# One network's first product by Strassen's scheme, in tiles of 256 tokens

## The chip, the cores and the metric

The kernel runs on one core of one Trainium2 chip. The metric is device time in microseconds (us) of one execution. Before the change three runs gave 991.76, 989.52 and 991.64 us; the median is 991.64 us.

## The reference

Attention over 4 x 576 = 2304 tokens gives x of 2304 x 512, and two networks follow it.

```python
# attention: a pooled part (factor 4) plus a local part (|i - j| < 4), summed
x = (out_up + out_local).transpose(0, 2, 1, 3).reshape(2304, 512)
# first network, 1536 wide
g = x @ w_gate
x = (g / (1 + exp(-g)) * (x @ w_val)) @ w_out
# second network, 2048 wide
h = np.maximum(x @ w_in, 0.0)
out = h * h @ w_out
```

The weights arrive as 64-bit floats and every product is to have about fp32 accuracy.

## The kernel before

Every operand of a product is split into a high and a low part (tiles `w`, `xh`, `hh`, type fp32r), and one product of a 128-row block is three matmuls: high by high, high by low, low by high. `proj` (lines 929 to 931) does the first products of both networks, with a block of weights as the stationary operand and the tokens of a tile as the moving one: 4 row blocks x 3 = 12 matmuls for one block of 128 columns. `down` (939 to 941) is the second product of the first network. The second product of the second network (1232 to 1234) holds 128 tokens of `hh` and moves 512 columns of weights.

The work has four stages on TensorE. Attention runs first, woven into the first one below. **B1** does units 0 to 5 of the first network's 12 units (a unit is 128 of the 1536 columns: gate, value, down, 36 matmuls): six tiles of 256 tokens, then two of 384; tiles 0 and 1 do units 4 and 5 later, under the name R. **B2** does units 6 to 11 in six tiles of 384 and adds the partial result that B1 spilled. **C** is the second network: six tiles of 384 tokens by 16 units, 12 matmuls of 384 columns and 9 of 512 in each.

VectorE (DVE) and ScalarE (ACT) turn the 64-bit weights into the two parts (`w_task`, lines 271 to 309: one ACT operation, three DVE operations on bits, one ACT copy, one DVE subtraction, each 128 x 512), split x (892, 898), and do the steps between two products (960 to 982 in the first network; 1212 to 1222 in the second). All loads and spills are issued by SyncE's queue (SP), in the order of its program; a load stands there until its buffer is free.

The order on every engine is fixed when the program is built, by a planner in the code (`Order`): it keeps a clock for each engine, gives every step a cost (`dve`, `act`, `products`, `dma`), and takes next the step that can begin first, by due times where several can. Until its clock says 40 us it puts matmuls on zeros (`fill`, line 1124) where TensorE would have nothing to do. Buffers are counted in `free`; a step that takes one waits in the plan until one is given back.

Of the kernel before, what the change touches and what calls it, by code (L numbers as in the profile page):

```python
# [23 lines left out]
WIN = 64  # L24
# [5 lines left out]
T2 = 384  # L30

X_WIDE = 6
X_AT = [*range(0, X_WIDE * T1, T1), *range(X_WIDE * T1, NTOK + 1, T2)]
NT1 = len(X_AT) - 1
NT2 = NTOK // T2
# [26 lines left out]
def attn_moe_kernel(ctx: ExitStack, tc: tile.TileContext, qT, kT, vw, vin, vp, qp, kp, qs, ks, vs, maskc, masks, identc, wB, wC, out):  # L62
# [60 lines left out]
    class Order:  # L123
        def __init__(self):
            self.flying = []
            self.queues = {k: [] for k in ("x", "qk", "sum", "rows", "v", "att", "w", "mlp", "other")}
            n = {"att": N_ATT, "y": N_Y, "gv": N_GV, "p": N_P, "pt": N_PT, "v": N_V, "xt": N_XT}
            n |= {"wst": N_WST, "wf": N_WF, "w1": NW1, "w2": NW2, "xh": N_XH, "sg": N_SG, "hh": N_HH, "ys": 1}
            self.free = {k: [0.0] * c for k, c in n.items()}
            self.clock = {e: 0.6 for e in "vaptd"}  # L130
            self.load, self.filler, self.streak, self.landed = {}, None, 0.0, 0.0
# [33 lines left out]
        def start(self, task):  # L165
# [7 lines left out]
            for k in set(s.take):  # L173
                slots, n = sorted(self.free[k]), s.take.count(k)
                if len(slots) < n:
                    return None
                t = max(t, slots[n - 1])
# [28 lines left out]
        def run(self):  # L206
            while self.flying or any(self.queues.values()):
# [7 lines left out]
                for k in s.take:  # L215
                    self.free[k].remove(min(self.free[k]))
# [23 lines left out]
                for k in s.give:  # L240
                    self.free[k].append(t)
# [10 lines left out]
    w1_pool = tc.alloc_tile_pool(name="w1", bufs=1, side="right")  # L252
    pools = {"w1": w1_pool}
    w_tiles, w_tasks = {}, {}

    def w_task(key, src, slot, due, cond=None):

        u = {}

        def load():  # L260
            if key[1] == 0:
                w_tiles[key[0]] = pools[slot].tile(
                    [128, 2, 3, 512], F32R, tag=slot, bufs={"w1": NW1, "w2": NW2}[slot], name=slot
                )
            u["hi"], u["lo"] = (w_tiles[key[0]][:, i, key[1], :] for i in range(2))
            u["st"] = com.tile([128, 512, 2], I32, tag="wst", bufs=N_WST, name="wst")
            nc.sync.dma_start(out=u["st"], in_=src)

        def scale():
            u["f"] = com.tile([128, 512], I32, tag="wf", bufs=N_WF, name="wf")  # L270
            nc.scalar.activation(
                out=u["f"].bitcast(F32), in_=u["st"][:, :, 1].bitcast(F32), func=AF.Abs, scale=2.0**-112
            )

        def exponent():
            nc.vector.tensor_scalar(
                out=u["f"],
                in0=u["f"],
# [6 lines left out]
        def sign():  # L285
            nc.vector.scalar_tensor_tensor(
                out=u["f"],
                in0=u["st"][:, :, 1],
                scalar=-0x80000000,
                in1=u["f"],  # L290
                op0=ALU.bitwise_and,
                op1=ALU.bitwise_or,
            )

        def last_bits():
            nc.vector.scalar_tensor_tensor(  # L296
                out=u["f"],
                in0=u["st"][:, :, 0],
                scalar=29,
                in1=u["f"],  # L300
                op0=ALU.logical_shift_right,
                op1=ALU.bitwise_or,
            )

# [3 lines left out]
        def low():  # L308
# [38 lines left out]
    def pool_rows(b, which, half, h):  # L347
        src, dst = (k_t, kd_t) if which == "k" else (q_t, qd_t)
        if b not in dst:

            room = com.tile([128, KD, T2], F32, tag="ys", name="ys").rearrange("p k n -> p (k n)")
# [25 lines left out]
    def pool_v(b):  # L377

        us = [None] * HP

        def load(g):
            if g % 2 == 0:
                new = w1_pool.tile([128, 2, 3, 512], F32R, tag="w1", bufs=NW1, name="w1").bitcast(F32)
                us[g : g + 2] = [new[:QC, i, :2].rearrange("p c n -> p (c n)") for i in range(2)]
# [11 lines left out]
        for g in range(HP):  # L396
            stage = Stage("d", dma(QC * 1024), lambda g=g: load(g), ("w1",) if g % 2 == 0 else ())
            loads.append(Task([stage], x_due(0) - 9.0))
            give = ("w1",) if g % 2 else ()
# [7 lines left out]
    def x_tile(t):  # L407
        if t not in x_t:
            order.free["xt"].remove(min(order.free["xt"]))
            x_t[t] = com.tile([128, KD, T2], F32, tag="xt", bufs=N_XT, name="xt")  # L410
# [83 lines left out]
    def local_task(b, i, ins, due, bls=(0, 1), early=False):  # L494
# [5 lines left out]
        def room(k, size=None):  # L500
            if not early_room:
                early_room.append(com.tile([128, 2 * KD * T2], F32, tag="xh", bufs=N_XH, name="xh"))
            return early_room[0][:, k * 256 : k * 256 + (size or n * WIN)]
# [9 lines left out]
        def scores():  # L513
# [4 lines left out]
            if early:  # L518
                u["p"] = room(2 * i).rearrange("p (c k) -> p c k", k=WIN)
# [50 lines left out]
        def turned():  # L570
            u["pt"] = room(5 + 2 * i) if early else att.tile([128, 512], F32, tag="pt", bufs=N_PT, name="pt")[:, : n * WIN]
# [62 lines left out]
        if early:  # L634
            p_take, pt_take, pt_give = ("xh",) * first, (), ("xh",) * last
# [241 lines left out]
    xh_t, x_tasks, y_t, ys_t, downs = {}, {}, {}, {}, []  # L877

    def x_task(key, n, load=None, cond=None, give=()):
# [9 lines left out]
        def high(k0):  # L889
            if k0 == 0:  # L890
                xh_t[key] = com.tile([128, 2, KD, T2], F32R, tag="xh", bufs=N_XH, name="xh")
            nc.scalar.activation(
# [527 lines left out]
```

## Time and profile before

| what | value |
|---|---|
| median of 3 runs (lowest to highest) | 991.64 us (989.52 to 991.76) |
| span of the profiled execution | 989.6 us |
| TensorE matmul (PE), busy | 976.9 us, 99% |
| VectorE (DVE), busy | 546.8 us, 55% |
| ScalarE (ACT), busy | 371.8 us, 38% |
| mean granted TensorE clock | 0.996 |
| moved by DMA | 100.11 MB |

For the profiled execution there is its span, from the first instruction to the last, and no other time. The lowest run, 989.52 us, is not above it, so nothing can be seen that lies around the span; the median is 2.0 us above it.

A matmul's listed time runs from its start to the modelled end of its results, and the next one starts long before that. How long one really takes is therefore read from the distance between starts. B1 with attention ends at about 287 us, B2 at about 591 us, C at 985 us.

### The profile page before, as it was taken

The page shows a single profiled execution, that of the slowest core. Times are in us where ns is not written, and L with a number is a line of the kernel's source. Part 1 is how long each engine was busy: PE and PEld are TensorE (multiplying, and loading weights), DVE is VectorE, ACT ScalarE, POOL GpSimd, SP SyncE. Part 2 cuts the span into 40 slices and gives each one's busy share as a digit, 9 for nine tenths or more (in the row PEclk, how much of TensorE's full clock was granted, in tenths as well). Part 3 has the DMA queues.
Part 4 walks back from the last instruction along what each step waited for, and adds up shares of the span by engine and source line. Part 5 has one row for each costly group of instructions (what it writes and reads, how often), then busy time and mean ns, then how long its engine had stood idle before and what let it go on. Part 6 is the DMA issues. An engine that isn't in the chain of part 4 may idle for free.

```text
span 989.6 us, 17229 instructions
## 1 busy us (share of the span) xinstructions
PE 976.9 (99%) x7122; PEld 915.8 (93%) x7122; DVE 546.8 (55%) x1163; ACT 371.8 (38%) x844; POOL 23.8 (2%) x31
## 2 busy tenths in 40 slices
PE   8989999999999999999999999999999999999998
PEld 7868999999999999999999999999999999999996
DVE  6999996559589698542342598532322322322222
ACT  3676663443355355221121255432322322322222
POOL 0202020000000000000000000000000000000000
PEclk9989999999999999999999999999999999999999
DMA  9989785142473555220320554010100000000000
GB/s 274 265 269 266 209 185 137 44 123 51 145 251 112 185 183 174 96 90 7 96 74 23 167 177 160 20 64 1 32 32 1 20 14 1 32 1 1 33 1 32
DMA packets 67770, 100.11 MB, mean 101 GB/s; under 512 B 19564, under 2 KB 51820, under 8 KB 67692
## 3 DMA queue, kind: packets, MB, share of 16 engines
q1 hardware_dynamic: 64236, 91.04, 29.1%
q0 software_dynamic: 3456, 7.96, 4.7%
q8 instruction: 56, 0.92, 0.4%
q14 instruction: 22, 0.18, 0.1%
HBM read 79.07 MB, written 19.92 MB: 100 GB/s over the span
## 4 chain that ended last, share of the span: by engine, by line
PE 97%; DVE 1%; DMA 1%; ACT 1%; SPq 0%; issue 0%
PE gv L929 17%; PE gv L931 17%; PE gv L930 17%; PE att L1234 5%; PE att L1232 5%; PE att L1233 4%; PE y L939 4%; PE y L941 3%; PE y L940 3%; PE y L1233 2%; PE y L1232 2%; PE y L1234 2%; PE att L527 2%; PE att L585 2%; PE att L939 2%; PE att L941 2%
## 5 line engine op out<-in xcount | busy, mean ns | idle before, releaser
L929 PE MATMUL gv<-xh,w 128*128 128x384 f32 (+1 forms) x1056 | 342.8, 325 | 0.0
L931 PE MATMUL gv<-xh,w 128*128 128x384 f32 (+1 forms) x1056 | 339.6, 322 | 0.0
L930 PE MATMUL gv<-xh,w 128*128 128x384 f32 (+1 forms) x1056 | 339.1, 321 | 0.0
L929 PEld LDWEIGHTS gv<-xh,w 128*128 128x128 f32 x1056 | 199.0, 188 | 6.0 <-issue 0.6
L930 PEld LDWEIGHTS gv<-xh,w 128*128 128x128 f32 x1056 | 199.1, 189 | 3.9
L931 PEld LDWEIGHTS gv<-xh,w 128*128 128x128 f32 x1056 | 199.0, 188 | 0.2 <-DVE w L309 0.2
L1222 DVE TENSOR_TENSOR hh<-sg,hh 128x384 fp32r<-128x384 f32 x96 | 53.6, 558 | 124.4 <-ACT hh L1219 124.4
L1215 DVE TENSOR_TENSOR sg<-sg 128x384 f32<-128x384 f32 x96 | 53.6, 558 | 116.0 <-ACT sg L1212 115.9
L1219 ACT ACTIVATE hh<-sg 128x384 fp32r<-128x384 f32 x96 | 50.4, 525 | 128.5 <-PE y L1234 126.4
L1212 ACT ACTIVATE sg<-gv 128x384 f32<-128x384 f32 x96 | 47.1, 491 | 132.5 <-PE gv L931 131.0
L973 DVE SCALAR_TENSOR_TENSOR sg<-sg,gv 128x384 f32<-128x384 f32 (+1 forms) x84 | 41.7, 496 | 95.3 <-PE gv L931 94.4
L979 ACT ACTIVATE hh<-sg 128x384 fp32r<-128x384 f32 (+1 forms) x84 | 40.0, 476 | 132.1 <-DVE sg L973 131.6
L1234 PE MATMUL att<-w,hh 128*128 128x512 f32 x192 | 76.0, 396 | 0.0
L1232 PE MATMUL att<-w,hh 128*128 128x512 f32 x192 | 75.7, 394 | 0.0
L1233 PE MATMUL att<-w,hh 128*128 128x512 f32 x192 | 75.6, 394 | 0.0
L939 PE MATMUL y<-hh,w 128*128 128x256 f32 (+1 forms) x240 | 74.5, 310 | 0.0
L941 PE MATMUL y<-hh,w 128*128 128x256 f32 (+1 forms) x240 | 72.7, 303 | 0.1
L940 PE MATMUL y<-hh,w 128*128 128x256 f32 (+1 forms) x240 | 72.5, 302 | 0.0
L968 DVE SCALAR_TENSOR_TENSOR sg<-sg,gv 128x384 f32<-128x384 f32 (+1 forms) x84 | 41.5, 494 | 43.6 <-ACT sg L960 42.9
L960 ACT ACTIVATE sg<-gv 128x384 f32<-128x384 f32 (+1 forms) x84 | 37.3, 444 | 68.3 <-PE gv L931 68.1
L306 ACT ACTIVATE w<-wf 128x512 fp32r<-128x512 f32 x68 | 42.8, 629 | 41.0 <-DVE wf L296 40.5
L982 DVE TENSOR_TENSOR hh<-sg,hh 128x384 fp32r<-128x384 f32 (+1 forms) x84 | 41.8, 498 | 19.1 <-ACT hh L979 18.9
(97 smaller groups left out, 1356.2 us busy)
## 6 DMA issues: line engine op xcount, KB each, us to landing
wst<-wB SPq DMA_DIRECT2D x36, 512.0 KB, 4.2
wst<-wC SPq DMA_DIRECT2D x32, 512.0 KB, 3.9
y_sp<-ys SPq DMA_DIRECT2D x8, 768.0 KB, 3.8
xt<-x_sp SPq DMA_DIRECT2D x6, 768.0 KB
ys<-y_sp SPq DMA_DIRECT2D x6, 768.0 KB, 4.7
xt<-y_sp SPq DMA_DIRECT2D x6, 768.0 KB, 5.3
out<-ys SPq DMA_DIRECT2D x17, 256.0 KB, 2.1
qT<-qT SPq DMA_DIRECT2D x7, 592.0 KB, 9.9
```

The source lines that it names most:

```text
L929: nc.tensor.matmul(ps[:, :n], w[:, 0], xh[:, 0, kk, :n], start=(kk == 0), stop=False)
L930: nc.tensor.matmul(ps[:, :n], w[:, 0], xh[:, 1, kk, :n], start=False, stop=False)
L931: nc.tensor.matmul(ps[:, :n], w[:, 1], xh[:, 0, kk, :n], start=False, stop=(kk == KD - 1))
L939: nc.tensor.matmul(y, w[:, 0], hh[:, 0, :n], start=start, stop=False)
L940: nc.tensor.matmul(y, w[:, 0], hh[:, 1, :n], start=False, stop=False)
L941: nc.tensor.matmul(y, w[:, 1], hh[:, 0, :n], start=False, stop=stop)
L1215: nc.vector.tensor_tensor(out=u["r"], in0=u["r"], in1=u["r"], op=ALU.mult)
L1219: nc.scalar.activation(out=u["h"][:, 0], in_=u["r"], func=AF.Copy)
L1222: nc.vector.tensor_tensor(out=u["h"][:, 1], in0=u["r"], in1=u["h"][:, 0].bitcast(F32), op=ALU.subtract)
L1232: nc.tensor.matmul(o, u["h"][:, 0, c], w[:, 0], start=(f == 0), stop=False)
L1233: nc.tensor.matmul(o, u["h"][:, 0, c], w[:, 1], start=False, stop=False)
L1234: nc.tensor.matmul(o, u["h"][:, 1, c], w[:, 0], start=False, stop=last)
```

## The change

All tiles have 256 tokens, so B1 and B2 have nine tiles each. B2's sums take the two `att` banks of PSUM and the two `y` banks in turn. In C two neighbouring tiles form a pair of 512 tokens, which makes four pairs and a single tile that is left over. Two neighbouring blocks of 128 columns form a unit `q`, of which there are eight. For a pair and a unit the first product is a 2 x 2 by 2 x 2 block product, done by the Strassen-Winograd scheme with seven products P1 to P7 of six matmuls instead of eight. Four operands are sums or differences of weight blocks (S1 to S4, formed in fp32 before the split), four are sums or differences of token blocks (T1 to T4). P2, P3 and P4 are accumulated on top of P1, P5 and P7 in PSUM after DVE or ACT has read these; DVE adds the results up. The single tile uses four products in place of the four that it had.

Weights of a unit now take six slots (four for the first product, two for the second). Six of the eight units are converted during B2, stored to DRAM (`w_sp`) and fetched again when they are needed. C makes three visits: units 0 to 3 for pairs 0, 1, 2 and the single tile, all eight units for pair 3, and then units 4 to 7 for pairs 0, 1, 2 and the single tile. The partial results of the first visit are stored (`y2_sp`) and added at the end of the third.

The core of the diff, with lines left out:

```diff
-T2 = 384
-X_WIDE = 6
-X_AT = [*range(0, X_WIDE * T1, T1), *range(X_WIDE * T1, NTOK + 1, T2)]
+X_AT = [*range(0, NTOK + 1, T1)]
...
-N_ATT, N_Y, N_GV, N_P, N_PT, N_V, N_XT, N_WST, N_WF, N_XH, N_SG, N_HH = 4, 2, 2, 5, 2, 2, 2, 3, 3, 2, 2, 2
+N_ATT, N_Y, N_GV, N_P, N_PT, N_V, N_XT, N_WF, N_SG, N_HH = 4, 2, 2, 5, 2, 2, 2, 5, 2, 3
-NW1, NW2 = 6, 5
+NAMED = {"wg": (18, 13), "xs": (4, 5), "wst": (4, 0)}
+KEEP_AT = 2
...
+    ya = ("att", "att")
+    for t in range(NT1):
+        x_task(("B2", t), T1, lambda t=t: load_x(x_sp, t), lambda t=t: after([spills[t]]), ("xt",))
+        tags = ya if t % 2 == 0 else y2
...
+        first = Task(
+            [Stage("d", d, lambda: load(0), ("wst", "wf", "wf") + ("wg",) * 4, cond=lambda: after([late_]))]
+            + read(0)
+            + [
+                Stage("a", act(512), high0),
+                Stage("v", dve(512), low0),
+                Stage("v", dve(256), combine(s3, a11, a21, ALU.subtract), cond=lambda: after([second])),
+                Stage("v", dve(256), combine(a21, a21, a22, ALU.add)),
+                Stage("v", dve(256), combine(s2, a21, a11, ALU.subtract)),
+                Stage("v", dve(256), combine(s4, a12, s2, ALU.subtract), (), ("wf",)),
...
+    for q in range(KEEP_AT, 2 * NFP):
+        convert(q)
+        put_by([("U", q, i) for i in range(4)], w_tasks["U", q, 0])
...
+    for q in range(KEEP_AT, 2 * NFP):
+        for key in [("U", q, i) for i in range(4)] + [("D", q, i) for i in range(2)]:
+            fetch(key)
...
+    def product(o, w, x, start, stop, more):
+        for kk in range(2):
+            three(o[:, :T1], w[:, :, kk * 128 : kk * 128 + 128], x[:, :, kk], start and kk == 0, stop and kk == 1, more)
...
+            pe("P1", "x1", "A11", "B11", True, True, ("gv",))
+            pe("P6", "x2", "S2", "T2", True, True, ("gv",))
+            pe("P5", "z", "S1", "T1", True, True, ("y",))
+            pe("P7", "y", "S3", "T3", True, True, ("y",))
+            pe("P2", "x1", "A12", "B21", False, True, (), [lambda: at(mid, 0)()])
+            pe("P3", "z", "S4", "B22", False, True, (), [lambda: at(mid, 2)()])
+            pe("P4", "y", "A22", "T4", False, True, (), [lambda: at(mid, 3)()])
...
+                    Stage("a", act(T1, True), begin, ("sg", "rr"), (), lambda: after([steps["P1"]])),
+                    Stage("v", d, add(s, "x2", s), (), ("gv",), lambda: after([steps["P6"]])),
+                    Stage("v", d, add(lambda: r(3), "z", s), (), (), lambda: after([steps["P5"]])),
+                    Stage("v", d, add(lambda: r(3), "y", lambda: r(3)), (), (), lambda: after([steps["P7"]])),
+                    Stage("v", d, add(lambda: r(1), "z", s), (), ("y",), lambda: after([steps["P3"]])),
+                    Stage("v", d, add(lambda: r(2), "y", s), (), ("y", "sg"), lambda: after([steps["P4"]])),
...
+    visits = [(0, g, halves_[0]) for g in (*range(turn), NPAIRS)]
+    visits += [(2, turn, range(2 * NFP))]
+    visits += [(1, g, halves_[1]) for g in (*range(turn), NPAIRS)]
```

**TensorE at the start of the program**, from attention's first tile (line 585, in the changed kernel 600) to the first product of the first network. Line 674 (690) is the pooled scores, 1124 (1143) a matmul on zeros. Before:

```order
L585 MATMUL att_529<-xh_132 64x56 x7
L674 MATMUL att_539<-ys_93,qT_380 72x144 [waits DMAHW4_49,PE_49,Activation_49]
...
L674 MATMUL att_567<-ys_93,qT_380 72x144 [waits DVE_49]
...
L929 MATMUL gv_603<-xh_562,w1_260 128x256 [waits Activation_49]
L930 MATMUL gv_603<-xh_562,w1_260 128x256 [waits DVE_49]
```

With the change:

```order
L600 MATMUL att_540<-xs_137 64x56 x7
L1143 LDWEIGHTS zeros_78
L1143 MATMUL y_107<-zeros_78 128x256
...
L690 MATMUL att_593<-ys_95,qT_426 72x144 [waits DMAHW5_49,PE_49,Activation_49]
...
L938 MATMUL gv_615<-xs_556,wg_266 128x256 [waits Activation_49]
L939 MATMUL gv_615<-xs_556,wg_266 128x256 [waits DVE_49]
...
L690 MATMUL att_645<-ys_95,qT_426 72x144 [waits PE_49]
```

27 matmuls on zeros now stand ahead of the pooled scores, and the second half of these scores has moved behind the network's first 12 matmuls.

**TensorE in the middle of C**, one unit. Lines 929 to 931 (938 to 940) are the first product, 1232 to 1234 (1634 to 1636) the second, of the unit before. Before:

```order
L929 MATMUL gv_8641<-xh_8048,w1_5208 128x384 [waits Activation_49]
...
L931 MATMUL gv_8641<-xh_8048,w1_5208 128x384
L1232 MATMUL att_8626<-w1_5100,hh_8623 128x512 [waits Activation_49]
L1233 MATMUL att_8626<-w1_5100,hh_8623 128x512
L1234 MATMUL att_8626<-w1_5100,hh_8623 128x512 [waits DVE_49]
...
L929 MATMUL gv_8670<-xh_8048,w1_5336 128x384 [waits Activation_49]
```

With the change, a row from the head of each block of matmuls (P6, P5, P7, second product, P2, second product, P3, P4):

```order
L938 MATMUL gv_10125<-xs_9746,wg_8356 128x256 [waits Activation_49]
...
L938 MATMUL y_10141<-xs_9734,wg_8339 128x256 [waits DVE_49]
...
L938 MATMUL y_10151<-xs_9763,wg_8356 128x256 [waits DVE_49]
...
L1634 MATMUL att_10058<-wg_7643,rh_10134 128x512 [waits Activation_49]
...
L938 MATMUL gv_10114<-xs_9765,wg_8323 128x256 [waits Activation_49]
...
L1634 MATMUL att_10058<-wg_7664,rh_10134 128x512 [waits Activation_49]
...
L938 MATMUL y_10141<-xs_9768,wg_8371 128x256
...
L938 MATMUL y_10151<-xs_9900,wg_8339 128x256 [waits DVE_49]
```

The two halves of the unit before's second product (12 matmuls each) now stand between P5 or P7 and the products P3 and P4 that are accumulated on the same banks.

**SyncE's queue in B2**, where weights of the second network are loaded (`wst<-wC`). Before:

```order
L267 DMA wst<-wC 128x1024 x2
L1038 DMA ys<-y_sp 128x4x384
L267 DMA wst<-wC 128x1024 x6
L1173 DMA xt<-x_sp 128x4x384
L1045 DMA y_sp<-ys 512x1x384
```

With the change, one tile's worth:

```order
L1068 DMA y_sp<-ys 512x1x256
L1221 DMA wst<-wC 128x1024 x2
L316 DMA wst<-wC 128x1024 x2
L1061 DMA ys<-y_sp 128x4x256
L1307 DMA w_sp<-wg 128x1024 x3
L1307 DMA w_sp<-wg 256x1x256
L1307 DMA w_sp<-wg 128x1024 x2
L1157 DMA xt<-x_sp 128x4x256
```

Six stores of converted weights per unit `q` now stand in this queue between the loads and stores of the tiles.

## Rows read from the trace of the kernel before

**Rows 1.** The page: busy time and share of engines; clock in 40 slices.
```profile
PE 976.9 (99%) x7122; PEld 915.8 (93%) x7122; DVE 546.8 (55%) x1163; ACT 371.8 (38%) x844; POOL 23.8 (2%) x31
PEclk9989999999999999999999999999999999999999
```

**Rows 2.** The page: chain that ended last, shares of the span.
```profile
PE 97%; DVE 1%; DMA 1%; ACT 1%; SPq 0%; issue 0%
```

**Rows 3.** Timeline, PE, 256 columns: start, us; ends of three unbroken runs.
```profile
152.10 0.28 PE L930 MATMUL gv<-xh,w 128*128 128x256 f32 x1
...
171.80 0.28 PE L931 MATMUL gv<-xh,w 128*128 128x256 f32 x1
...
172.88 0.28 PE L940 MATMUL y<-hh,w 128*128 128x256 f32 x1
...
185.32 0.28 PE L941 MATMUL y<-hh,w 128*128 128x256 f32 x1
...
258.63 0.28 PE L940 MATMUL y<-hh,w 128*128 128x256 f32 x1
...
279.76 0.28 PE L931 MATMUL gv<-xh,w 128*128 128x256 f32 x1
```

**Rows 4.** Timeline, PE, B2: ends of a run of 384 columns.
```profile
439.68 0.33 PE L930 MATMUL gv<-xh,w 128*128 128x384 f32 x1
...
473.73 0.34 PE L941 MATMUL y<-hh,w 128*128 128x384 f32 x1
```

**Rows 5.** Timeline, PE, C: a unit's blocks, and eight units on.
```profile
700.12 0.39 PE L1232 MATMUL att<-w,hh 128*128 128x512 f32 x1
...
702.20 0.33 PE L929 MATMUL gv<-xh,w 128*128 128x384 f32 x1
...
704.30 0.39 PE L1232 MATMUL att<-w,hh 128*128 128x512 f32 x1
...
733.58 0.40 PE L1232 MATMUL att<-w,hh 128*128 128x512 f32 x1
```

**Rows 6.** Timeline, PE, start: matmuls on zeros, then the pooled scores.
```profile
28.57 1.27 PE L1124 MATMUL y<-zeros 128*128 128x256 bf16 x10
...
32.24 4.55 PE L674 MATMUL att<-ys,qT 64*72 64x144 f32 x64
```

**Rows 7.** Windows: stretch, length, busy by engine (count), clock, DMA share, GB/s.
```profile
37.00:140.00 103.00, 98.50 (x1266) 87.36 (x1265) 96.45 (x268) 69.30 (x214) 13.82 (x16) 0.97 0.91 243
53.00:68.00 15.00, 10.52 (x140) 8.17 (x138) 14.19 (x44) 10.19 (x33) 0.00 (x0) 1.00 0.92 285
68.00:75.00 7.00, 6.98 (x50) 5.62 (x52) 5.82 (x14) 5.03 (x19) 0.84 (x1) 0.52 0.76 182
280.00:310.00 30.00, 30.00 (x183) 30.00 (x182) 26.18 (x49) 16.18 (x30) 0.00 (x0) 1.00 0.73 235
800.00:900.00 100.00, 100.00 (x503) 90.39 (x502) 28.87 (x51) 26.97 (x52) 0.00 (x0) 1.00 0.02 9
```

**Rows 8.** Timeline, C: ACT and DVE after a first product.
```profile
704.50 0.49 ACT L1212 ACTIVATE sg<-gv 128x384 f32<-128x384 f32 x1 [1.58 <-PE gv L931]
...
705.02 0.56 DVE L1215 TENSOR_TENSOR sg<-sg 128x384 f32<-128x384 f32 x1 [1.51 <-ACT sg L1212]
```

**Rows 9.** Groups by form: busy us, mean ns; DVE and ACT by size.
```profile
L309 DVE TENSOR_TENSOR w<-wf,w 128x512 fp32r<-128x512 f32 x68 | 46.7, 688 | 8.4 <-ACT w L306 7.7 <-issue 0.2
...
L306 ACT ACTIVATE w<-wf 128x512 fp32r<-128x512 f32 x68 | 42.8, 629 | 41.0 <-DVE wf L296 40.5
...
L982 DVE TENSOR_TENSOR hh<-sg,hh 128x256 fp32r<-128x256 f32 x36 | 15.1, 420 | 5.1 <-ACT hh L979 5.1
```

**Rows 10.** C's end: the timeline's last matmul, then the chain's last copies.
```profile
984.47 0.40 PE L1234 MATMUL y<-w,hh 128*128 128x512 f32 x1
...
984.91 0.39 ACT ys L1299
...
985.32 0.42 DVE ys L1297
```

More of the change, by code (lines that the diff above doesn't have):

```diff
@@ L173, in start @@
             for k in set(s.take):
-                slots, n = sorted(self.free[k]), s.take.count(k)
+                slots, n = sorted(t_ for t_, _ in self.named[k]) if k in self.named else sorted(self.free[k]), s.take.count(k)
                 if len(slots) < n:
@@ L634, in local_task @@
         if early:
-            p_take, pt_take, pt_give = ("xh",) * first, (), ("xh",) * last
+            p_take, pt_take = ("xs",) * 3 * first, ()
+            pt_give = tuple(lambda k=k: ("xs", early_room[k][0]) for k in range(3)) if last else ()
         task = Task(
@@ L991, in out_ @@
                 ]
-            down(y_t[name, ti], w_tiles[j], u["h"], n, first, last)
+            down(y_t[name, ti], w_tiles[j, 2], u["h"], first, last)
         def gate_cond():
@@ L1198, in c_unit @@
+    y2_stores = {}
+    last_down = [downs[-1]]
+    def c_unit(ps_, g, q, qs, spent):
+        key = "C", ps_, g
+        single = g == NPAIRS
+        n = T1 if single else 2 * T1
+        nsub = n // 128
+        first, last = q == qs[0], q == qs[-1]
         u = {}
@@ L1236, in evacuate, with pe, go, ready @@
-        def evacuate(i):
-            if i == 0:
-                ys_t["C", t] = com.tile([128, NSUB, DM], F32, tag="ys", name="ys")
-            os_ = ys_t["C", t]
+        steps = {}
+        prev = last_down[0]
+        def pe(name, ps, w, x, start, stop, take=(), cond=()):
+            def go():
+                if start:
+                    u[ps] = bank(take[0])
+                product(u[ps], factor(q, w), xh_t[key][x], start, stop, not (start or single))
+            before = list(steps.values())[-1:]
+            def ready():
+                if any(s.at == 0 for s in before):
+                    return None
+                needs = [f() for f in cond] + [after([x_tasks[key][x], w_tasks["U", q, UP[w][0]]])]
+                return None if None in needs else max(needs)
+            give = ((lambda: ("xs", x_at[key][x])),) * (last and free_x.get(name, False))
+            steps[name] = Task([Stage("t", PROD, go, take, give + w_free_of(name), ready)], due + 0.01 * len(steps), True)
@@ new lines, in c_begin, with load @@
+    def c_begin(ps_, g, nsub, r0, due, task):
+        if ps_ != 1:
+            return
+        def load(h):
+            yc_t[ps_, g, h] = block_tile("yc")
+            src = y2_sp[r0 + 2 * h : r0 + 2 * h + 2].rearrange("r p d -> p r d")
+            nc.sync.dma_start(out=yc_t[ps_, g, h], in_=src)
+        before = yc_out[0]
+        for h in range(nsub // 2):
+            needs = [y2_stores[g, h], *before]
+            yc_in[g, h] = Task(
+                [Stage("d", dma(128 * 1024), lambda h=h: load(h), ("yc",), (), lambda n=needs: after(n))], due, True
+            )
+            task.then = [*task.then, yc_in[g, h]]
@@ new lines, in c_end @@
+        end = []
+        tight = g == NPAIRS
+        for i in range(nsub):
+            cuts = [slice(0, DM // 2), slice(DM // 2, DM)] if tight and i == nsub - 1 else [every]
+            for k, c in enumerate(cuts):
+                give = ("att",) * (k == len(cuts) - 1)
+                size = c.stop - c.start
+                t = Task(
+                    [Stage("v", dve(size), add(i, c), (), give, lambda i=i: after([task, yc_in[g, i // 2]]))], due + 0.6, True
+                )
+                if tight:
+                    t.stages.append(Stage("d", dma(128 * size), lambda i=i, c=c: put(i, c)))
+                made.append(t)
```

697 lines of the change are left out of this document (478 added, 219 removed).

## The prediction

> **What bounds the kernel now.** I read the page's busy times first and then its chain of waits. Matmuls are listed as busy for 99% of the span [rows 1], and the chain that ended last runs through TensorE for 97% of it [rows 2]. The listed busy time says little by itself, since a matmul's listed time overlaps the next one's; so I took the timeline and looked for unbroken starts. In the stretch of C from 800 to 900 us TensorE has no idle time, while VectorE is busy for 28.87 of 100 us and DMA for 2% [rows 7]. In B2 the starts run on without a break as well [rows 4]. Only the first part is different: from 37 to 140 us TensorE is busy for 98.50 of 103 us, VectorE for 96.45 and DMA for 91% [rows 7]. So from about 140 us on the time is the number of matmuls times the distance of their starts, and anything done by other engines costs nothing as long as it keeps up.
>
> **The prices.** With 256 columns the three unbroken runs give (171.80 - 152.10) / 166 = 0.1187, (185.32 - 172.88) / 106 = 0.1174 and (279.76 - 258.63) / 178 = 0.1187 us per matmul [rows 3]; together 53.27 / 450 = 0.1184. With 384 columns B2 gives (473.73 - 439.68) / 196 = 0.1737 us [rows 4]. A unit of C takes (733.58 - 700.12) / 8 = 4.18 us, of which the 12 matmuls of 384 take 704.30 - 702.20 = 2.10 us; so the 9 of 512 take 0.2314 us each [rows 5]. Per column this is 0.463 ns with 256, 0.452 with 384 and 0.452 with 512: small tiles are dearer by 2.4%.
>
> **The change part by part, TensorE first.**
> - B1's last 768 tokens: 2 x 6 x 36 = 432 matmuls of 384 become 3 x 6 x 36 = 648 of 256. 75.0 us become 76.7: +1.7.
> - B2: 6 x 6 x 36 = 1296 become 9 x 6 x 36 = 1944. 225.1 become 230.2: +5.1.
> - C: 6 x 16 = 96 units of 4.18 us are 401.5 us. Now each of eight units q has 42 matmuls of 256 for each of four pairs and 24 for the single tile, 8 x (168 + 24) = 1536 in place of the 1728 of an ordinary product in such tiles: 181.9 us. The second product keeps its 864 matmuls of 512: 199.9 us. Together 381.8: -19.7.
>
> The sum is -12.9 us. Seen otherwise, the seventh product in place of the eighth saves 192 x 0.1184 = 22.7 us, and the smaller tiles give back 9.8. The 256-column price carries it: with 0.1174 for all 4128 new matmuls it is -17.0, with 0.1187 it is -11.7. I take 0.1184, the mean of all 450.
>
> The Trainium skill ("TensorE: Matmul & The Clock Gate", on the 56 against 53.3 ns) says that back-to-back matmuls at full clock start N / 2.4 GHz plus a fixed 2.5 ns or so apart, which would make tile size nearly free. By it 256, 384 and 512 columns would take 109, 163 and 216 ns, and the sum would be -17.2 us. The rows disagree: 118, 174 and 231 ns, an excess of 12, 14 and 18 ns over the bare columns, and I go by them.
>
> **The start.** The changed order puts 27 more matmuls on zeros ahead of the pooled scores. Ten of these took 1.27 us [rows 6], so 27 cost at most 3.4 us. Before, TensorE went straight on from attention's tile to the scores at 32.24 us without waiting. Later, between 53 and 68 us, TensorE stood idle for 15 - 10.52 = 4.5 us because attention's steps on VectorE were late [rows 7], and there a part of the lost time can be won back: the first product is late by 3.4, but if VectorE sets the pace it is not. Bounds -1 and +3.4; I take +2. After these gaps the granted clock fell to a mean of 0.52 for 7 us (1.2 in place of 2.4 GHz, after a stretch in which TensorE was busy for 70% of the time) [rows 7], a loss of some 3.4 us. The changed order has nearly the same attention steps between nearly the same products there; I count no difference, and keep -3.4 and +3.4 as bounds.
>
> **Waits in C.** Six matmuls of a product take 0.71 us. P2 is put on top of P1 after ACT has read it; P6, P5, P7 and half of the second product lie between. P3 and P4 wait for VectorE's additions, and the whole second product of the unit before (5.6 us) lies between. Nearest is the second product's first half behind P3: from rows of before, 0.20 us from TensorE to the next engine (ACT begins at 704.50, the next block at 704.30), 0.03 from ACT to DVE [rows 5, 8], then an addition 0.42, a square 0.69, a copy 0.63 [rows 9], some 2.1 us with the handovers. In the order P4 and four products stand between, 3.55 us. VectorE needs about 5 x 0.42 + 4 x 0.69 = 4.9 us for a unit of a pair and 11 x 0.69 = 7.6 us for the token sums of a pair, spread over four units of 10.5 us: about two thirds busy. So the steady state costs nothing. If a foreign operation of 0.69 us comes in twice, the cover is just gone. Where a visit changes to the next pair, all four banks of the result have to be emptied (two operations of 0.69 us one behind the other on VectorE, as much on ACT); the order puts ten products of the next pair there. I take 1.5 us for all eight changes. Bounds: nothing, as before, where no wait showed, and 8 us, the emptying laid bare each time with some waiting.
>
> **The end.** Before, the copy on ACT began 0.03 us after TensorE was done, and 0.83 us later the last copy was over [rows 10]. Now VectorE alone adds, a whole bank and two halves, about 0.6 + 0.33 + 0.42 = 1.35, and the last unit has only half of a second product to cover its chain. Together +1.0, bounds +0.3 and +2.
>
> **Conversion, stores and fetches.** VectorE gets four sums of 256 and one and a half more subtractions of 512 per unit q, 2.7 us each, 22 us in all, and all eight conversions now fall into B2. What hides it is B2's length; the nearest row is 280 to 310 us, where VectorE was listed at 26.18 of 30 us with no idle time on TensorE [rows 7]. DMA is closer to its limit: between the first and the sixth of B2's stores of y, SP's new order has 24 loads of 64-bit weights, 27.5 stores and 14.5 transfers of x and y, each of 0.52 MB. 34.6 MB in five tiles of 25.6 us are 270 GB/s. Rows show 285 GB/s at a share of 0.92 and 235 at 0.73 [rows 7], 310 to 322 at a full share. I count nothing, and the lack of cover is the second rival. The fetches in the long visit have three units of lead (31 us) for 2.9 MB each.
>
> **The sum.** -12.9 + 2 + 1.5 + 1.0 = -8.4 us against the span of 989.6: 981.2 us. The median of the runs is 2.0 us above that span, so I forecast 983.2 us.
>
> **The rivals.**
> 1. VectorE falls behind in B2. For it: all conversion is there, and its operations stand in one queue with the steps between two products. If TensorE is idle in the proportion of 37 to 140 us, 4.5 of 103 [rows 7], over the seven tiles that conversion lasts (179 us), this is 7.8 us: 991 us, no change. Against it: 280 to 310 us.
> 2. DMA becomes the bound of B2. Stores of converted weights go through the same queue as the tiles' x and y, and conversions wait for their slots. It decides below 270 GB/s. From 68 to 75 us the rows had 182 at a share of 0.76, 240 at a full one [rows 7]; at that rate the five tiles take 144 us instead of 128: +16 us, 999 us, slower. Against it: this mixture had small packets of attention, the weights move in rows of 4 KB.
> 3. The 256-column price is 0.1174 throughout, fillers are won back, nothing waits in C: -17.0 - 1 + 0.3 = -17.7, 974 us.
>
> That the scheme doesn't do its work is no rival: the order has 4128 + 1296 matmuls of 256 (those of the first six tiles stay) and 864 of 512.
>
> **Chances.** Forecast 0.62 (its own range 977 to 988), rival 1 0.14, rival 2 0.12, rival 3 0.12. About 0.3%, 3 us, can be told from no change here, so 988.7 to 994.6 is "same": rival 1. Faster 0.74, same 0.14, slower 0.12. The range 974 to 995 leaves out half of rivals 2 and 3.
>
> **What would show it.** Starts of 256-column matmuls 0.118 us apart in B2 and C; C some 20 us shorter, B2 some 5 longer; the first product of the first network near 37.5 us instead of 36.7. Idle TensorE in B2 with DVE as the releaser speaks for rival 1, DVE itself waiting for `wst`, and SP's stores standing, for rival 2. I am wrong if new idle time on TensorE sums to more than 12 us, or if accumulating on a bank just read makes the starts slower.

## The result, and the profile after

| kernel | median, us (lowest to highest) | ratio to before (95% interval) |
|---|---|---|
| before, beside it | 990.62 (989.52 to 991.76) | 1 |
| changed | 980.21 (979.31 to 980.72) | 0.9892 (0.9878 to 0.9906) |

The changed kernel is faster by 1.1%, clear of noise. The forecast was 983.2 us. The profiled execution of the changed kernel has a span of 978.6 us and a time of 980.34, so 1.7 us lie around the span; in all runs of this case it is 1.7 to 1.9 us. So the 2.0 us between median and span in the section on the time before, where nothing around the span could be seen, are mostly time of that kind.

The page of the changed kernel, busy times, clock and chain of waits, against [rows 1, 2]:

```profile
PE 968.0 (99%) x8397; PEld 907.4 (93%) x8397; DVE 668.2 (68%) x1500; ACT 385.3 (39%) x926; POOL 24.2 (2%) x31
...
PEclk9998999999999999999999999999999999999999
...
PE 97%; DVE 1%; ACT 1%; issue 0%; DVEq 0%; ACTq 0%
```

TensorE still bounds the kernel. VectorE has 121 us more to do and ends no later for it. The windows, with the columns of [rows 7]:

```profile
37.00:60.00 23.00, 22.09 (x273) 19.34 (x271) 21.32 (x62) 14.11 (x47) 2.34 (x3) 0.93 0.92 274
60.00:80.00 20.00, 16.64 (x209) 14.46 (x208) 18.87 (x53) 14.66 (x48) 1.32 (x2) 0.83 0.90 270
...
370.00:520.00 150.00, 150.00 (x1257) 149.66 (x1256) 127.90 (x274) 68.95 (x147) 0.00 (x0) 1.00 0.78 266
800.00:900.00 100.00, 100.00 (x629) 90.07 (x629) 62.04 (x118) 28.70 (x59) 0.00 (x0) 1.00 0.19 64
```

In B2, where all conversions now stand, TensorE is listed as busy for 150.00 of 150 us, with VectorE at 127.90 and DMA at a share of 0.78.

Where the time went is seen by counting matmuls: lines 938 to 940 do 1944 of them in B1, 1944 in B2 and 1536 in C (before, lines 929 to 931 and 939 to 941: 1728, 1296 and 1152), so in the changed kernel the 1945th and the 3889th start B2 and C. From the timelines of the kernels, in us (the rows from the third on are the experiments below; "apart" is the distance in bytes between the addresses of a matmul's two operands):

| kernel | first product | B2 starts | B2 | C, to TensorE's end | after it | span |
|---|---|---|---|---|---|---|
| before | 36.7 | 357.6 | 225.2 | 402.0 | 4.8 | 989.6 |
| changed | 36.5 | 359.7 | 232.3 | 382.6 | 4.0 | 978.6 |
| 27 fillers left out | 34.3 | 358.9 | 232.2 | 382.6 | 4.0 | 977.8 |
| P6 twice | 36.6 | 359.9 | 232.3 | 405.2 | 4.0 | 1001.4 |
| more VectorE work | 36.7 | 358.5 | 245.1 | 382.6 | 4.0 | 990.2 |
| stores twice | 36.7 | 359.9 | 310.0 | 382.6 | 4.2 | 1056.7 |
| operands 64 apart | 36.7 | 353.0 | 222.6 | 376.1 | 4.0 | 955.7 |
| operands 0 apart | 36.3 | 361.9 | 233.6 | 382.2 | 4.0 | 981.7 |
| operands 64 and 192 apart | 39.0 | 353.5 | 222.7 | 376.9 | 4.0 | 957.1 |
| 64 apart, 27 fillers left out | 33.9 | 352.8 | 223.8 | 376.1 | 4.0 | 956.7 |
| before, 64 apart | 35.6 | 352.3 | 226.0 | 400.1 | 4.8 | 983.3 |

Up to B2 the change costs 2.1 us, in B2 7.0; C gives 19.4 and the end 0.7: -11.0 us of span.

The start on TensorE's timeline answers to [rows 6]: the 27 added matmuls on zeros, the first half of the pooled scores, and the network's first product.

```profile
31.13 3.12 PE L1143 MATMUL y<-zeros 128*128 128x256 bf16 x27
34.18 2.41 PE L690 MATMUL att<-ys,qT 64*72 64x144 f32 x32
36.52 0.39 PE L938 MATMUL gv<-xs,wg 128*128 128x256 f32 x1
```

The first product is no later than before, since the scores' second half now stands behind it. The prices (the time from one start to the next), against [rows 3, 4], are the ends of two unbroken runs of 256 columns (TensorE's timeline at the turn of B1 to B2, and in B2):

```profile
290.11 0.28 PE L939 MATMUL gv<-xs,wg 128*128 128x256 f32 x1
...
356.87 0.28 PE L938 MATMUL gv<-xs,wg 128*128 128x256 f32 x1
...
541.90 0.29 PE L938 MATMUL gv<-xs,wg 128*128 128x256 f32 x1
...
559.18 0.28 PE L938 MATMUL gv<-xs,wg 128*128 128x256 f32 x1
```

66.76 us over 569 matmuls are 0.1173 us, 17.28 over 144 are 0.1200. That is the same instruction at two prices, without a pause in either run. All of the first run's weights lie in the pool that was there from the start, all of the second's in the pool opened after attention. Over the whole trace from 290 us on, B2 and C alike, the old pool's weights go at 0.1173 to 0.1178 us and the new pool's at 0.1196 to 0.1200.

The end, against [rows 10], as the timeline has it: the last matmul, and VectorE's adding and copying.

```profile
973.88 1.45 DVE L1697 TENSOR_TENSOR yc<-att,yc 128x512 f32<-128x512 f32 x3 [0.60 <-PE att L1636]
...
974.14 0.40 PE L1636 MATMUL att<-wg,rl 128*128 128x512 f32 x1
```

The first of the three additions began 0.66 us before TensorE was done (974.54), so only 0.79 us of the 1.45 lie behind it.

### The profile page after: what moved, and what is told of

Its sections match the earlier page's. It is cut to its first block, busy times and chain, and to the rows that moved or that the text cites. A ratio compares the mean times of both kernels' runs of the same rounds, so it can differ in the third digit from the quotient of the medians.

```text
span 978.6 us, 20467 instructions
## 1 busy us (share of the span) xinstructions
PE 968.0 (99%) x8397; PEld 907.4 (93%) x8397; DVE 668.2 (68%) x1500; ACT 385.3 (39%) x926; POOL 24.2 (2%) x31
## 4 chain that ended last, share of the span: by engine, by line
PE 97%; DVE 1%; ACT 1%; issue 0%; DVEq 0%; ACTq 0%
PE gv L938 14%; PE gv L940 13%; PE gv L939 13%; PE y L938 7%; PE y L940 7%; PE y L939 7%; PE att L1634 7%; PE att L1635 7%; PE att L1636 7%; PE att L542 2%; PE att L600 2%; PE y L1143 2%; PE att L690 2%; PE att L939 2%; PE att L938 1%; PE att L940 1%
## 5 line engine op out<-in xcount | busy, mean ns | idle before, releaser
L938 PE MATMUL gv<-xs,wg 128*128 128x256 f32 x1120 | 318.0, 284 | 0.0
L939 PE MATMUL gv<-xs,wg 128*128 128x256 f32 x1120 | 314.9, 281 | 0.0
L940 PE MATMUL gv<-xs,wg 128*128 128x256 f32 x1120 | 314.9, 281 | 0.0
L938 PEld LDWEIGHTS gv<-xs,wg 128*128 128x128 f32 x1120 | 212.3, 190 | 3.3 <-DVE sg L987 0.2
L939 PEld LDWEIGHTS gv<-xs,wg 128*128 128x128 f32 x1120 | 212.4, 190 | 2.0
L940 PEld LDWEIGHTS gv<-xs,wg 128*128 128x128 f32 x1120 | 212.3, 190 | 0.0
L1634 PE MATMUL att<-wg,rh 128*128 128x512 f32 x288 | 113.7, 395 | 0.0
L1635 PE MATMUL att<-wg,rh 128*128 128x512 f32 x288 | 113.5, 394 | 0.0
L1636 PE MATMUL att<-wg,rl 128*128 128x512 f32 x288 | 113.2, 393 | 0.0
L993 ACT ACTIVATE hh<-sg 128x256 fp32r<-128x256 f32 x108 | 44.8, 415 | 118.0 <-DVE sg L987 113.5
L938 PE MATMUL y<-hh,wg 128*128 128x256 f32 x312 | 90.9, 291 | 0.0
L1606 ACT ACTIVATE rh<-rr 128x512 fp32r<-128x512 f32 (+1 forms) x80 | 46.8, 588 | 108.0 <-DVE rr L1599 107.5
L939 PE MATMUL y<-hh,wg 128*128 128x256 f32 x312 | 88.6, 284 | 0.0
L940 PE MATMUL y<-hh,wg 128*128 128x256 f32 x312 | 88.5, 284 | 0.0
L987 DVE SCALAR_TENSOR_TENSOR sg<-sg,gv 128x256 f32<-128x256 f32 x108 | 45.2, 418 | 56.7 <-PE gv L940 55.5
L982 DVE SCALAR_TENSOR_TENSOR sg<-sg,gv 128x256 f32<-128x256 f32 x108 | 45.1, 418 | 39.6 <-ACT sg L974 39.2
L940 PE MATMUL y<-xs,wg 128*128 128x256 f32 x256 | 72.0, 281 | 0.0
L939 PE MATMUL y<-xs,wg 128*128 128x256 f32 x256 | 71.9, 281 | 0.0
L938 PE MATMUL y<-xs,wg 128*128 128x256 f32 x256 | 71.9, 281 | 0.0
L1636 PEld LDWEIGHTS att<-wg,rl 128*128 128x128 f32 x288 | 54.1, 188 | 12.8 <-DVE rl L1609 0.2
```

The lines of the kernel that those rows point to most:

```text
L938: nc.tensor.matmul(o, w[:, 0], x[:, 0], start=start, stop=False, skip_group_check=more)
L939: nc.tensor.matmul(o, w[:, 0], x[:, 1], start=False, stop=False, skip_group_check=more)
L940: nc.tensor.matmul(o, w[:, 1], x[:, 0], start=False, stop=stop, skip_group_check=more)
L982: nc.vector.scalar_tensor_tensor(out=u["s"], in0=u["s"], scalar=1.0, in1=u["g"][:, :n], op0=ALU.add, op1=ALU.mult)
L987: nc.vector.scalar_tensor_tensor(out=u["s"], in0=u["s"], scalar=0.5, in1=u["v"][:, :n], op0=ALU.mult, op1=ALU.mult)
L993: nc.scalar.activation(out=u["h"][:, 0], in_=u["s"], func=AF.Copy)
```

## The experiments

What was open: whether the scheme's gain in C is the plain number of matmuls, whether the fillers lie on the path, how near the two rivals in B2 were, and why one matmul has two prices. Unless said otherwise an experiment is the changed kernel with one edit, and, apart from what the edit adds or leaves out, the sequence of every engine is as it was. Diffs show the core of an edit.

**The number of matmuls in C.**

```diff
+                if name == "P6":
+                    product(u[ps], factor(q, w), xh_t[key][x], True, True, False)
                 product(u[ps], factor(q, w), xh_t[key][x], start, stop, not (start or single))
...
-            steps[name] = Task([Stage("t", PROD, go, take, give + w_free_of(name), ready)], due + 0.01 * len(steps), True)
+            steps[name] = Task([Stage("t", PROD * (2 if name == "P6" else 1), go, take, give + w_free_of(name), ready)], due + 0.01 * len(steps), True)
```

The second part of the edit tells the planner that P6 takes twice as long. So in C it places the same steps of VectorE and ScalarE, and one fetch, in another order; this is the one experiment with a new order.

> The product P6 is computed twice on the same bank, so that a pair and unit take eight products as without the scheme: 32 x 6 = 192 more matmuls of 256 columns, while everything VectorE and ScalarE do stays. Theory A (in C the time is the number of matmuls times the distance of their starts): 192 x 0.1184 = 22.7 us more than the changed kernel, about 1003 us, all of it in C. Theory B (C waits in part for VectorE's additions or the emptying of banks, and the extra matmuls fill such waits): less than 20 us more.

Measured: 1003.06 us, ratio 1.0121 (1.0107 to 1.0135), 22.9 us above the changed kernel; B2 as it was, C longer by 22.6. Theory A holds: C has no waits that an added product would fill. The run also splits the result. With eight products in tiles of 256, and all of the scheme's additions and stores still in place, the kernel is 11 to 12 us slower than before; seven products in place of eight give 22.9.

**The fillers.**

```diff
-                self.filler()
+                if self.n_fill < 98:
+                    self.filler()
+                self.n_fill += 1
```

> The 27 additional matmuls on zeros at the start are left out (98 as in the kernel before), all else in the order of the changed kernel. The prediction counted them at +2 us (bounds -1 and +3.4). Theory A (the stretch up to 75 us waits for attention's steps on VectorE, and the lost time was won back): the time stays within 0.5 us of the changed kernel, 980 us, and the first product of the first network starts at 36 to 36.8 us. Theory B (they lie on the path): the first product starts at 33.6 us in place of 36.75 and the time falls by 2 to 3.4 us, 977 to 978 us. Against leaving them out: the granted clock could be lower in the first 40 us.

Measured: 979.38 us, ratio 0.9878 (0.9864 to 0.9891). The first product begins 2.3 us earlier, B2 only 0.8. The trace of this run, 37 to 80 us:

```profile
37.00:60.00 23.00, 19.89 (x265) 16.95 (x264) 21.91 (x63) 15.30 (x49) 2.56 (x3) 1.00 0.99 293
60.00:80.00 20.00, 17.48 (x214) 15.40 (x215) 18.74 (x53) 14.40 (x46) 0.84 (x1) 0.83 0.83 247
```

From 37 to 60 us TensorE is idle for 3.11 us instead of 0.91: most of what comes early waits for attention. The granted clock of this stretch is 1.00 instead of 0.93, so two effects are mixed in what is left. The figures lie between the theories: the first product is early, as theory B says (33.6), and the time falls by 0.8 us, nearer to theory A's 0.5 than to theory B's 2 to 3.4. So the fillers cost at most some 0.8 us, which is within what runs differ by.

**VectorE's cover in B2 (rival 1).** `n_sign` is 2 for the second network's weights:

```diff
         def sign():
+          for _ in range(n_sign):
             nc.vector.scalar_tensor_tensor(
```

> One of VectorE's operations on bits (0.686 us) is done twice in each of the 32 conversions of the second network's weights: 22 us more work for VectorE in B2, where it was busy for 127.9 of 150 us from 370 to 520 us. The result is the same and the order unchanged. Theory A (VectorE keeps up as long as it is below full): busy about 144 of 150 us, TensorE without idle time, within 2 us of the changed kernel, 979 to 982 us. Rival 1 of the prediction (steps between two products wait behind conversions): TensorE idle in B2 by 5 us or more, 985 us or more.

Measured: 993.61 us, ratio 1.0026 (1.0017 to 1.0035), 13.4 us above the changed kernel. Theory A fell. B2 is 12.8 us longer. Window, TensorE's waits from 360 to 605 us, and one of them as TensorE and VectorE list it (in this kernel lines 943 to 945 are the products, 992 the multiplication between two of them, 297 the doubled operation):

```profile
370.00:520.00 150.00, 143.51 (x1174) 140.71 (x1173) 133.97 (x281) 63.16 (x138) 0.00 (x0) 1.00 0.74 254
```

```profile
PE gv L943 <- DVE sg L992: 4.9, 7, 1.0
PE att L944 <- DVE hh L1001: 2.8, 6, 0.8
PE gv L943 <- DVE sg L987: 0.2, 1, 0.2
```

```profile
464.63 0.28 PE L945 MATMUL gv<-xs,wg 128*128 128x256 f32 x1
465.90 0.39 PE L943 MATMUL gv<-xs,wg 128*128 128x256 f32 x1 [0.99 <-DVE sg L992]
```

```profile
463.16 1.41 DVE L297 SCALAR_TENSOR_TENSOR wf<-wst,wf 128x512 int32<-128x512 int32 x2
464.49 0.42 DVE L1244 TENSOR_TENSOR wf<-wf 128x256 f32<-128x256 f32 x1
464.83 0.68 DVE L302 SCALAR_TENSOR_TENSOR wf<-wst,wf 128x512 int32<-128x512 int32 x1
465.43 0.42 DVE L992 SCALAR_TENSOR_TENSOR sg<-sg,gv 128x256 f32<-128x256 f32 x1
```

VectorE is not full, at 133.97 of 150 us, and still TensorE waits: the step that frees a bank stands behind conversion work in one queue, here behind 2.3 us of it, of which the edit added 0.69. The listed waits are 7.9 us. A break costs more than is listed, since a matmul counts as busy for 0.28 us where the next could start after 0.118: from 464.63 to 465.90 it is 1.27 - 0.12 = 1.15 us for 0.99 listed. Added up in this way over the timeline, 40 breaks make 13.3 us. In the changed kernel the same sum in B2 is 0.5 us. So rival 1's mechanism is real, and at most 22 us of VectorE's work away; no run brackets it closer.

**SyncE's queue in B2 (rival 2).**

```diff
                 nc.sync.dma_start(out=w_sp[at][:, :, :n], in_=w_tiles[key][:, :, :n].bitcast(F32))
+                nc.sync.dma_start(out=w_sp[at][:, :, :n], in_=w_tiles[key][:, :, :n].bitcast(F32))
```

> Every store of converted weights to DRAM is issued twice in a row (30 more transfers of 0.52 MB, 15.7 MB, between 350 and 540 us); all else as in the changed kernel. From 370 to 520 us the changed kernel moved 266 GB/s at a share of 0.78. Theory A (DMA has room there and the conversions have slack before their weights are needed): within 2 us of the changed kernel, 979 to 982 us, at 330 to 350 GB/s. Rival 2 of the prediction (DMA becomes the bound of B2): 48 + 15.7 MB at 341 GB/s (266 / 0.78) take 186 us where 180 are there, and waits of SP's queue for slots add to it: 986 us or more, TensorE idle in B2.

Measured: 1058.39 us, ratio 1.0682 (1.0667 to 1.0696). Longer as rival 2 says, by far more than it says, and not for its reason. (The expectation counted 30 stores; 36 are doubled, six of them half as large, and DMA moves 17.3 MB more.) Window, and SP's waits from 380 to 600 us:

```profile
370.00:520.00 150.00, 116.03 (x902) 114.20 (x900) 85.84 (x186) 47.26 (x102) 0.00 (x0) 0.89 0.70 245
```

```profile
SPq L1308 <- DMA w_sp<-wg: 152.2, 36, 9.2
```

DMA moves less than in the changed kernel (245 GB/s against 266). The second store goes to the same place as the first, and the program makes it wait in SP's queue, by a semaphore, until the first has landed. So the edit added 36 waits to the queue besides the bytes. One chain, in the lists of SP, ScalarE, VectorE and TensorE:

```profile
437.34 0.69 SPq L1307 DMA_DIRECT2D w_sp<-wg  x1
442.95 0.32 SPq L1308 DMA_DIRECT2D w_sp<-wg  x1
443.36 0.52 SPq L1068 DMA_DIRECT2D y_sp<-ys  x1
443.93 1.99 SPq L1221 DMA_DIRECT2D wst<-wC  x2
```

```profile
450.19 0.66 ACT L279 ACTIVATE wf<-wst 128x512 f32<-128x512 f32 x1 [13.09 <-DMA wst<-wC]
```

```profile
437.14 0.42 DVE L996 TENSOR_TENSOR hh<-sg,hh 128x256 fp32r<-128x256 f32 x1 [0.48 <-ACT hh L993]
450.88 0.43 DVE L282 TENSOR_SCALAR wf<-wf 128x512 int32<-128x512 int32 x1 [13.32 <-ACT wf L279]
451.23 0.41 DVE L982 SCALAR_TENSOR_TENSOR sg<-sg,gv 128x256 f32<-128x256 f32 x1
```

```profile
441.64 0.28 PE L940 MATMUL att<-hh,wg 128*128 128x256 f32 x1
451.70 0.58 PE L938 MATMUL gv<-xs,wg 128*128 128x256 f32 x1 [9.78 <-DVE sg L982]
```

The loads of 64-bit weights stand behind the waiting store. ScalarE's first step of their conversion waits for them for 13.09 us, VectorE's next instruction waits for that step for 13.32 us, with the network's own step behind it, and TensorE stands for 9.78 us. So the run doesn't tell how much bandwidth is left, and rival 2 as the prediction states it, a lack of bandwidth, stays untested. What the run shows is how a stop of SP's queue reaches TensorE, at a DMA share of 0.70.

**Why one matmul has two prices.** First an unused tile of 32, 1024 or 1888 bytes at the head of the new pool moved all its slots:

```diff
         post = tc.alloc_tile_pool(name="post", bufs=1)
+        post.tile([128, 8], F32, tag="pad", bufs=1, name="pad")
```

> An unused tile of 32 bytes per partition is put first in the new pool of weight slots, so that these slots start at 32 modulo 64 bytes as the old pool's do; the order of all engines is that of the changed kernel. In the changed kernel matmuls of 256 columns started 0.1198 to 0.1200 us apart where their weights lay in the new pool (0 modulo 64) and 0.1173 where they lay in the old one (32 modulo 64). Theory A (alignment to 64 bytes sets the distance): the new pool's distance falls to 0.1173 to 0.1175, B2 loses 3 to 4 us, C 1 to 3, the time is 4 to 6 us below the changed kernel, 974 to 976 us. Theory B (the residue modulo 2048, or the region of the memory): no change, 980 us, distance 0.1198 to 0.1200 as before.

> The same with an unused tile of 1024 bytes: the slots stay at 0 modulo 64 bytes, at 1152 in place of 128 modulo 2048. Theory A (alignment to 64 bytes): nothing changes, 980 us. Theory B1 (residue modulo 2048): the distance may become any value, faster only if 1152 is a good residue. Theory B2 (region): nothing changes, 980 us.

> The same with 1888 bytes: the slots of the new pool get the old pool's residue, 2016 modulo 2048, and so 32 modulo 64. Theory A (alignment to 64) and theory B1 (residue modulo 2048) both expect 0.1173 to 0.1175 us in both pools and 974 to 976 us. Theory B2 (region of the memory) expects no change, 980 us and 0.1198 to 0.1200 us in the new pool.

Measured: 979.48 us (ratio 0.9881, 0.9866 to 0.9896), 980.66 (0.9900, 0.9883 to 0.9917) and 980.43 (0.9888, 0.9874 to 0.9901). No kernel is told from the changed one by its time, so theories A and B1 fell as they stood. But the prices moved. With 1024 bytes they were as before; with 1888 both pools came to 0.118 to 0.119. With 32 the old pool, whose addresses had not changed, had two prices: 0.1156 to 0.1165 us where the tokens lay in the moved pool, 0.1174 to 0.1180 where they lay elsewhere. So it is not the weights' address alone that counts but its distance from the tokens'. From here on the address distance is the stationary operand's address minus the moving one's, modulo 128 bytes. Sorted by it, the traces of the changed kernel and these three gave 0.1191 to 0.1200 us for 0, 0.1185 for 32, 0.1156 to 0.1165 for 64, 0.1174 for 96: theory C, tested by setting the address distance everywhere. For 64, with the tokens' slots taken first:

```diff
+    for i in range(18):
+        pools["wg"][0].tile([128, 2, 512], F32R, tag=f"wg{i}", bufs=1, name="wg")
+    pools["wg"][0].tile([128, 8], F32, tag="pad", bufs=1, name="pad")
...
         post = tc.alloc_tile_pool(name="post", bufs=1)
+        for i in range(4, 9):
+            post.tile([128, 2, 2, T1], F32R, tag=f"xs{i}", bufs=1, name="xs")
+        post.tile([128, 16], F32, tag="pad", bufs=1, name="pad")
```

For 0 the old pool's slots are taken in the same way with a pad of 96 bytes, and the new pool stays as it was.

> The order of all engines is that of the changed kernel; only addresses move: every slot of weights starts at 64 modulo 128 bytes, every tile of tokens at 0 modulo 128, so the two operands of a 256-column matmul are 64 apart modulo 128. In the four runs so far the distance of starts went with (address of the stationary operand minus address of the moving one) modulo 128: 0 gave 0.1191 to 0.1200 us, 32 gave 0.1185, 64 gave 0.1156 to 0.1165, 96 gave 0.1174. Theory C (this difference sets the distance): 0.116 us in all of B2 and C, which makes B2 about 1944 x 0.0026 = 5 us shorter than in the changed kernel, C 1536 x 0.0022 = 3.4, B1 1600 x 0.0012 = 2: about 970 us. Theory D (chance of these runs, or another property of the slots): within 2 us of the changed kernel, 978 to 982 us.

> The counterpart: every slot of weights and every tile of tokens at 0 modulo 128 bytes, difference 0, order unchanged. Theory C: 0.1195 to 0.1200 us everywhere, 2 + 2 + 4 = 8 us longer than the changed kernel, about 988 us. Theory D: 978 to 982 us.

Measured: 957.5 us (ratio 0.9671, 0.9657 to 0.9686) with 64, 984.66 (0.9931, 0.9919 to 0.9943) with 0. Theory C holds in its direction, not in its sizes: with 64 the gain is 22.7 us where it said 10, and with 0 the kernel loses 4.5 where it said 8, since C came out no longer (382.2 us against 382.6). TensorE's timeline with 64, an unbroken run and then a piece further on:

```profile
290.08 0.28 PE L941 MATMUL y<-hh,wg 128*128 128x256 f32 x1
...
378.82 0.28 PE L941 MATMUL att<-hh,wg 128*128 128x256 f32 x1
...
410.39 0.33 PE L941 MATMUL gv<-xs,wg 128*128 128x256 f32 x1
410.56 0.28 PE L942 MATMUL gv<-xs,wg 128*128 128x256 f32 x1
...
428.81 0.28 PE L941 MATMUL att<-hh,wg 128*128 128x256 f32 x1
429.14 0.39 PE L942 MATMUL att<-hh,wg 128*128 128x256 f32 x1
429.36 0.28 PE L943 MATMUL att<-hh,wg 128*128 128x256 f32 x1
...
478.12 0.28 PE L941 MATMUL att<-hh,wg 128*128 128x256 f32 x1
```

And with 0:

```profile
264.08 0.28 PE L942 MATMUL y<-hh,wg 128*128 128x256 f32 x1
...
441.07 0.28 PE L941 MATMUL att<-hh,wg 128*128 128x256 f32 x1
```

With 64 it is 88.74 / 783 = 0.1133 us, with 0 it is 176.99 / 1475 = 0.1200, for the same instructions. A second thing shows at 410 us: behind two starts that lie 0.17 us apart the price is (428.81 - 410.56) / 155 = 0.1177 until the next break, and (478.12 - 429.36) / 430 = 0.1134 again behind it. So at one address distance there are two steady paces, and a short stop can change from one to the other. The kernel before shows the same at 96: its three runs of [rows 3], 0.1187, 0.1174 and 0.1187, all lie at that distance, and between the first two stands a short piece of attention. With 0 everywhere the long runs all have 0.1200.

> The changed kernel's order with difference 64 modulo 256 in the old pool of weight slots and 192 modulo 256 in the new one. In the kernel that ran at 957.5 us both were 64 modulo 256. Theory C, period 128: both pools at 0.1137 to 0.1147 us, 957 us. Theory C, period 256 or more: the new pool's matmuls of 256 columns (13 of 18 weight slots in B2, about a third of C) differ, at up to 0.120 us, so up to 1287 x 1.1 x 0.006 + 500 x 0.006 = 11 us more, 968 us; or less than 957 if 192 is better still.

The edit is that of the kernel with 64, with 192 bytes in the new pool's pad. Measured: 958.71 us (0.9682, 0.9663 to 0.9701). Where the address distance is 192 modulo 256, TensorE's timeline in B2 has (369.80 - 356.20) / 120 = 0.1133 us again:

```profile
356.20 0.28 PE L941 MATMUL gv<-xs,wg 128*128 128x256 f32 x1
...
369.80 0.28 PE L941 MATMUL gv<-xs,wg 128*128 128x256 f32 x1
```

So 64 and 192 are alike, as a period of 128 bytes has it. The kernel before, in the same way:

```diff
+    for _ in range(NW1):
+        w1_pool.tile([128, 2, 3, 512], F32R, tag="w1", bufs=NW1, name="w1")
+    w1_pool.tile([128, 8], F32, tag="pad", bufs=1, name="pad")
...
         pools["w2"] = tc.alloc_tile_pool(name="w2", bufs=1)
+        pools["w2"].tile([128, 16], F32, tag="pad", bufs=1, name="pad")
```

> The kernel before with its order unchanged; only its weight slots move, so that every slot starts 64 bytes (modulo 128) from the tiles of tokens; there the differences were 96 (old pool) and 0 (pool opened after attention). It asks whether the kernel before has the same gain at hand, and whether matmuls of 384 and 512 columns follow the address too. Theory C1 (only short matmuls, 256 columns, feel it): B1's 256-column matmuls fall from 0.118 to 0.1146 us, about 1500 x 0.0034 = 5 us, and 384 columns stay at 0.1737 to 0.175: about 986 us. Theory C2 (all sizes feel the same 4 to 6 ns): 2800 more matmuls of 384 and 512 x 0.004 = another 11 us, about 975 us. Theory D (address has nothing to do with it): 991 us.

Measured: 986.68 us, ratio 0.9954 (0.9942 to 0.9967): theory C1. Of the 5.3 us by which B2 starts earlier, 1.1 lie ahead of the first product. TensorE's timeline of this run:

```profile
150.10 0.28 PE L933 MATMUL gv<-xh,w 128*128 128x256 f32 x1
...
168.23 0.28 PE L934 MATMUL gv<-xh,w 128*128 128x256 f32 x1
```

18.13 / 160 = 0.1133 us for 256 columns. With 384 columns the price over B2 is 226.0 / 1296 = 0.1744 us, where it was 225.2 / 1296 = 0.1738 at the address distances 0 and 96. With 512 columns it is 0.2303; the other traces have 0.2295 to 0.2346 in no order of the address distance. C is 1.9 us shorter than before and B2 0.8 longer, so nothing of the size that 256 columns show.

> The addresses of the kernel with difference 64 and, besides, the 27 additional matmuls on zeros at the start left out (a candidate for a version faster than both). Theory C: about 970 us, less 0 to 1 us for the start, where leaving them out alone gave 979.4 against 980.2 us. Theory D: 977 to 981 us.

Measured: 957.29 us, ratio 0.9660 (0.9647 to 0.9673), the fastest kernel here: 34 us below the kernel before and 23 below the changed one. Without the fillers or with them makes no difference that can be told.

## Why the prediction was right, step by step

- **TensorE bounds the kernel; other engines cost nothing while they keep up.** Right: no idle time on TensorE behind the first 75 us, and one added product in eight comes back in full.
- **C, -19.7 and 1.5 of waits.** Measured -19.4. The waits were not there: in C the starts leave their steady pace for 0.3 us in all. P2, P3 and P4 on banks just read made no start slower. That the price of 0.1184 fits C is luck: there about two thirds of the 256-column matmuls lie at an address distance of 96 and go at 0.1177, the rest lie at 0 and go at 0.1197, and the mean is 0.1184.
- **B2, +5.1.** Measured +7.0. This is the term that was mis-sized, by its price. I took 0.1184 us as one price with some scatter. In B2 it was 232.3 / 1944 = 0.1195, because 13 of the 18 slots of B2's weights lie at an address distance of 0 from the tokens and are paid at 0.1200. The rows before gave no hint of 0.1200: there all 256-column weights lay at 96, and the 384-column ones, which lay at 0 too, don't feel it. The scatter itself was no chance: 0.1187 and 0.1174 are the two paces at 96.
- **B1 and the start, +1.7 and +2.** Measured +2.1 together. The first product is not late: the prediction counted the fillers and not that half of the pooled scores moved behind it. Of the fillers' 3.1 us at most 0.8 come through. The clock cost somewhat more than before (a mean of 0.93 over 23 us and 0.83 over 20, 5.0 us lost against 3.4), inside the bounds that were kept.
- **The end, +1.0.** Measured -0.7. The three additions take 1.45 us where 1.35 was put, but the first lies beside the last matmuls: VectorE is done 0.79 us behind TensorE's end, where the copies were done 0.87 us behind it [rows 10]. The last stores then take 3.2 us instead of 3.9.
- **Rivals 1 and 2.** Neither came. But the cover that I named, a share of busy time, was not the measure: from 370 to 520 us VectorE at 85% hid everything, and asked to do 22 us more in B2 it came to 89% while TensorE waited. For DMA, 36 waits in the queue that it is issued from stopped TensorE at a share of 0.70; how near its bandwidth was to a bound stays open.
- **Rival 3.** Its total was 6 us too low: waits were absent as it says, but the price went up in B2, not to 0.1174.
- **The sum.** -8.4 us was forecast and -11.0 measured. The miss of B2, +1.9, was more than made up by three terms that were put too high: B1 and the start by 1.6, C with its waits by 1.2, the end by 1.7.

By the rule of the Trainium skill ("TensorE: Matmul & The Clock Gate", on the 56 against 53.3 ns) an estimate for 256 columns is 109 ns; the prediction's sum by it comes out at -17.4 us, not -17.2. The runs show 113 at the best addresses and 120 at the worst, so the measured price stays the one to go by, and it has to be taken at the operands' addresses.

## What to carry to other kernels

Where TensorE bounds a kernel, take the price of a matmul from unbroken starts, apart for each pool that its operands come from: if it differs, set the pools so that the two operands of short matmuls lie 64 bytes apart modulo 128, before anything else is rewritten. Moving one pool by 32 bytes changed prices here but not the time; 64 between all operands gave 22.7 us. Busy shares don't say how much more work another engine can hide: here TensorE waited for steps that stood behind foreign work in VectorE's queue while VectorE was at 89%. A store that has to wait for an earlier one to land holds up everything behind it in its queue.

## What the runs showed of the hardware

- Matmuls of 256 columns, fp32r, each with its own weights, start 0.1200 us apart where the stationary and the moving operand start at the same address modulo 128 bytes within a partition (down to 0.1191 as the mean of one kernel), 0.1173 to 0.1187 at 96, 0.118 to 0.1185 at 32 and 0.1133 or 0.1177 at 64. For this kernel the ends lie 27 us apart. With 384 and 512 columns no such difference showed.
- There are two steady paces at 64 (0.1133 and 0.1177) and at 96 (0.1173 and 0.1187), entered and left at short breaks. Why the address distance matters, and what chooses the pace, no run here tests: the cause is open.
